# A routed layer of seven tiles: from one written engine order to four

## The chip, the core and the metric

One core of a Trainium2 chip runs the whole program. The metric is the device time of one execution in microseconds (us), the median of several runs. Beside it stands one profiled execution, from which every row below is read. TensorE (PE, with its weight loads as PEld), VectorE (DVE), ScalarE (ACT), GpSimd (POOL) and SyncE (SP) each work through a queue of their own in order; semaphores tie the queues together.

## The reference, cut to what matters

Attention comes first, then a dense layer with a softplus, then the layer that the change touches. In it a score decides which tokens are computed at all, a gate sends each of them to one of eight experts, and the expert's output is scaled and added to the token:

```
do_compute = x @ w_skip > 0
xc = x[do_compute]                       # x: 1152 x 512
e_idx = argmax(xc @ w_gate, axis=1)      # 8 experts
gate_w = softmax(xc @ w_gate)[e_idx]
for e in range(8):
    mask = e_idx == e
    h = maximum(xc[mask] @ w1[e], 0)     # w1[e]: 512 x 1024
    y[mask] = gate_w[mask] * (h @ w2[e]) # w2[e]: 1024 x 512
out[do_compute] = xc + y                 # other tokens: out = x
```

## The kernel before, in words

**Tiles.** The routed tokens are put into tiles of 128 that all belong to one expert: T = 0 to 6. Tile 0 is computed inside `passage` (L800), which also works out the routing; tiles 1 to 6 are the loop in `tiles` (L1165). Rests of an expert with few tokens go into two small items, 0 and 1, of 32 tokens each.

**Weights.** A tile's expert has eight chunks of 128 x 1024 words. Chunks 0 to 3 are w1, chunks 4 to 7 are w2; they are loaded into eight fixed buffers `raw[0]` to `raw[7]` by SP (`load_chunk`, L945). The loads of tiles 1 to 6 carry a condition: where a tile has the same expert as the one before it, the instruction is run and its semaphore rises, but nothing is moved. Each `raw[c]` is one buffer for all tiles, so tile T+1's load of chunk c waits until tile T's readers of it are done.

**Splits.** Products are made exact by splitting each operand into a rounded part and a rest. `split_w` (L962) makes from `raw[c]` a tile `ws` of two halves: ACT casts the rounded part (L966, "cast"), DVE subtracts it to get the rest (L967, "low"). Chunk 0 is not split (`AS_IS`): it is multiplied as it stands, so its matmuls wait for the load of `raw[0]` itself.

**One tile.** Its tokens are fetched by an indirect DMA from POOL into `xg`, turned by four PE transposes (`gather`, L982: `xgt`), copied out by ACT (`xgw`, `xgT`) and DVE (`xgT`, low). The hidden phase multiplies by chunks 0 to 3 into `mh` (4 + 18 matmuls). ACT applies the relu (`hs`, L1022). PE turns `hs` in two halves (`ht`), which ACT and DVE split into `hT`. The result phase multiplies `hT` by chunks 4 to 7 into `y` (24 matmuls). DVE scales and adds (`yo`, L1059), and POOL scatters the rows (L1060); DVE makes its row numbers first (`si`, L1057). In the loop the result of tile T-1 stands behind the hidden phase of tile T.

**Small items.** `small_x` (turn the tokens, `sxt`), `small_hidden` (`smh`, 32 matmuls), `small_turn` (`sht`), `small_result` (`sy`, 64 matmuls; then `ssi`, L1121, and `syo` on DVE). Their weights go through four buffers `sraw`, loaded twice per item, 2 MB each time, without a condition. `SMALL` (L40) says at which tile each step stands.

**What sets the order.** `passage` runs under a manual schedule for PE, DVE, ACT and SP: the written order is the queue's order. `tiles` runs under a manual schedule for PE alone; DVE, ACT and SP are ordered by the scheduler of the language from a timeline that it estimates. `issue_after` pins a few of them. PSUM tiles `xgt`, `ht`, `sxt` and `sht` share two buffers (`ps_x`).

## Time and profile before

| | us |
|---|---|
| median of 3 runs | 516.83 (516.09 to 518.12) |
| profiled execution, its own time | 516.66 |
| its span in the trace | 514.9 |
| between span and time | 1.76 |
| tile 1's first matmul, from the span's start | 397.71 |
| last small result's end, last tile's result begins | 500.4 |

The profiled execution is 0.17 us under the median, so sums are made against it. Columns: a window row gives its bounds and length, then per engine busy us and instructions, the mean granted TensorE clock (1.00 is 2.4 GHz, 0.50 is 1.2 GHz), the DMA share and GB/s. A timeline row gives start, duration, engine, line, operation, output<-input, shapes and count; in brackets stand the idle time before it and what ended that. A wait row gives who waited for whom: us in total, times, the longest.

### The profile page before, as it was taken

Reading aid. Unit: us, or ns where it says so; the run is one execution under the profiler, and the core shown is the slowest. Engines: PE = TensorE matmul, PEld = TensorE weight load, DVE = VectorE, ACT = ScalarE, POOL = GpSimd, SP = SyncE. Lnnn points to the kernel's source line nnn. Section 1 sums busy time; section 2 is a strip of 40 time slices with the busy share of each in tenths; the row PEclk is TensorE's granted clock in tenths of the full one; section 3 lists DMA queues with packets and bytes.
Section 4 is the critical chain, followed back from the end, with each engine's and each line's share of the span. In section 5 each row is a group of like instructions: output and inputs, shape, how many; then the busy total and the mean of one; then the engine's idle time right before and its main releaser. Section 6 shows DMA issues by size and latency. Waiting matters only on the chain. (4 is left out here: it accounts for less than half of the span.)

```text
span 514.9 us, 8832 instructions
## 1 busy us (share of the span) xinstructions
PE 479.5 (93%) x3048; PEld 385.3 (75%) x3049; DVE 371.0 (72%) x697; ACT 331.1 (64%) x782; POOL 122.1 (24%) x167
## 2 busy tenths in 40 slices
PE   7999999998999999999999999999999589799893
PEld 3778777776676788999988998998975456577582
DVE  7676777689987977899898864468847347476882
ACT  2666776767766877877777767666734165464860
POOL 0966967565113200000000000011005200211111
PEclk9999999999999999999999999999999798899997
DMA  7568536746730412233333305003265841909001
GB/s 184 157 167 216 138 89 172 180 127 172 189 97 23 164 42 53 71 123 122 123 123 106 115 27 204 1 4 113 76 204 175 342 164 31 357 30 341 3 25 37
DMA packets 41509, 65.49 MB, mean 127 GB/s; under 512 B 9087, under 2 KB 23679, under 8 KB 41456
## 3 DMA queue, kind: packets, MB, share of 16 engines
q1 hardware_dynamic: 38480, 59.99, 38.1%
q0 software_dynamic: 1344, 4.20, 2.3%
q10 hardware_dynamic: 1632, 0.66, 0.6%
q8 instruction: 26, 0.43, 0.3%
q14 instruction: 27, 0.22, 0.1%
HBM read 67.32 MB, written 6.76 MB: 144 GB/s over the span
## 5 line engine op out<-in xcount | busy, mean ns | idle before, releaser
L590 PE MATMUL h<-xh,w 128*128 128x320 f32 (+2 forms) x464 | 104.2, 309 | 0.8 <-ACT rb L95 0.8
L628 PE MATMUL acc<-w,gh 128*128 128x512 f32 x288 | 80.7, 397 | 1.0 <-ACT gh L618 1.0
L590 PEld LDWEIGHTS h<-xh,w 128*128 128x128 f32 x464 | 78.1, 188 | 4.7 <-ACT rb L95 1.1
L590 PE MATMUL h<-xl,w 128*128 128x320 f32 (+2 forms) x232 | 69.2, 308 | 0.0
L269 DVE TENSOR_REDUCE m<-s 128x1 f32<-128x576 f32 x64 | 48.0, 754 | 19.9 <-PE s L260 16.2
L628 PEld LDWEIGHTS acc<-w,gh 128*128 128x128 f32 x288 | 51.8, 188 | 11.5 <-ACT gh L618 2.7
L967 DVE TENSOR_TENSOR ws<-raw,ws 128x1024 fp32r<-128x1024 f32 x42 | 49.9, 1220 | 7.8 <-ACT ws L966 7.3
L282 ACT ACTIVATE P<-s,m 128x576 f32<-128x576 f32 x64 | 47.6, 750 | 12.2 <-DVE m L269 11.9
L603 ACT ACTIVATE y<-h 128x320 f32<-128x320 f32 (+2 forms) x58 | 25.4, 438 | 41.1 <-PE h L590 39.9
L637 PE MATMUL y<-ws,hT 128*128 128x512 f32 x144 | 40.9, 427 | 8.5 <-ACT ws L966 6.1
L702 POOL TENSOR_SCALAR sc<-lg 128x2 f32<-128x2 f32 (+1 forms) x3 | 0.9, 291 | 201.3 <-DVE lg L685 201.3
L351 PE MATMUL t<-ct,P 128*128 128x128 f32 x288 | 45.6, 277 | 2.5 <-ACT pt L95 2.5
L628 PE MATMUL acc<-w,gl 128*128 128x512 f32 x144 | 45.9, 392 | 0.0
L260 PE MATMUL s<-ks,qs 128*128 128x288 f32 x224 | 43.7, 317 | 1.8 <-ACT P L282 1.8
L590 PEld LDWEIGHTS h<-xl,w 128*128 128x128 f32 x232 | 43.2, 188 | 2.1
L619 DVE TENSOR_TENSOR gl<-r,gh 128x256 fp32r<-128x256 f32 (+2 forms) x42 | 25.8, 614 | 26.1 <-ACT gh L618 25.9
L966 ACT CAST ws<-raw 128x1024 fp32r<-128x1024 f32 x42 | 42.1, 1066 | 3.0 <-issue 3.0
L637 PE MATMUL mh<-ws,xgT 128*128 128x512 f32 x132 | 37.8, 431 | 5.4 <-DVE ws L967 4.4
L351 PEld LDWEIGHTS t<-ct,P 128*128 128x128 f32 x288 | 33.6, 140 | 9.6 <-issue 3.5
L95 ACT COPY pt<-t 128x384 f32<-128x384 f32 x60 | 28.1, 480 | 18.4 <-PE t L351 18.2
L637 PEld LDWEIGHTS y<-ws,hT 128*128 128x128 f32 x144 | 27.2, 200 | 16.3 <-ACT ws L966 6.8
L395 PE MATMUL pv<-pt,vr 128*64 128x256 f32 (+1 forms) x256 | 37.1, 412 | 0.0
(305 smaller groups left out, 945.4 us busy)
## 6 DMA issues: line engine op xcount, KB each, us to landing
raw<-in_moe_w_dram SPq DMA_DIRECT2D x56, 512.0 KB
raw<-in_moe_w_in_dram SPq DMA_DIRECT2D x16, 512.0 KB
raw<-in_moe_w_out_dram SPq DMA_DIRECT2D x16, 512.0 KB
sraw<-in_moe_w_dram SPq DMA_DIRECT2D x16, 512.0 KB
ks<-kT SPq DMA_DIRECT2D x28, 288.0 KB
qs<-qT SPq DMA_DIRECT2D x28, 128.0 KB
wr<-in_moe_w_dram SPq DMA_DIRECT2D x5, 512.0 KB
x2d<-x SPq DMA_DIRECT2D x9, 256.0 KB
```

Of the source, the lines that this page charges most:

```text
L95: self.nc.scalar.copy(out, in_)
L260: nc.tensor.matmul(ps[:, c, 0:288], lhsT=qs[:, a, uc], rhs=ks[:, a, x, 288 * c : 288 * c + 288], start=x == 0, stop=x == 1,)
L269: self.last = nc.vector.tensor_reduce(st["m"][:, a : a + 1], st["ps"][a][:, :, 0:288], axis=AX.XY, op=ALU.max, negate=True)
L282: nc.scalar.activation(P[:, 576 * a : 576 * a + 576].rearrange("p (c n) -> p c n", c=2), ps[:, :, 0:288], AF.Exp, bias=m[:, a : a + 1], ac ...
L351: self.tail = nc.tensor.transpose(ps[:, 128 * i : 128 * i + 128], src, ident)
L395: nc.tensor.matmul(ps[r, 0:n], lhsT=v, rhs=pt[:, k, 0:n], start=i < 0, stop=i == 3, skip_group_check=True,)
L590: nc.tensor.matmul(ps[c][:, 0:m], lhsT=w[:, 0, x, 128 * k : 128 * k + 128], rhs=src[:, k, c0 + m * c : c0 + m * c + m], start=z == 0, stop ...
L619: self.last = nc.vector.tensor_sub(gl, r, gh.bitcast(F32))
L628: nc.tensor.matmul(acc[t], lhsT=g[x][:, 128 * j : 128 * j + 128], rhs=w[:, 1, y, :], start=f == f0 and z == 0, stop=f == f1 and z == 2,)
L637: mm()
L966: hi = nc.scalar.copy(w[:, 0], raw)
L967: self.did[T, c] = hi.ins, nc.vector.tensor_sub(w[:, 1], raw, w[:, 0].bitcast(F32)).ins
```

## The change

`tiles` is put under the manual schedule of all four engines, and its body is rewritten so that every cast, low, load and copy has a written place. The casts and lows of chunks 1 and 2 of tile T+1 and of chunks 5 to 7 of tile T-1 stand during tile T's hidden phase ahead of the relu, chunk 3 of T+1 behind it, chunk 4 of T in the middle of the result phase. The loads follow in the order in which their buffers come free: 5, then 0 of the next tile, 6 and 7, then 1 to 3 of the tile after the next, then 4 of the next. `passage` loads chunks 1, 2, 0 ahead of the routing's values and 3 and 4 behind, and takes over the first splits of tile 1. The transposes of the next tile's tokens (`rows`) move from behind the hidden phase into it, ahead of chunk 3; `gather` is cut into `rows` (PE) and `copies` (ACT and DVE). Tile 1's `ht` halves stand inside tile 2's hidden phase. The small items' tokens and hidden products come one tile later (tiles 2 and 5), the hidden product behind the result phase there; the turned product and result of item 0 move to tile 3, those of item 1 stay at tile 6. The row numbers `ssi` are made with their `syo`. The first loads of item 0 move into tile 1, those of item 1 into tile 4. `yo` and `si` of a tile are written behind the next hidden phase's matmuls. The fetched tokens of a small item get two buffers. The small helpers are cut in the same way into a PE part and a copy.

```diff
@@ -35,7 +35,7 @@
 FAR = 4096.0
 
 FULL = 7
-SMALL = {1: ("x0", "h0"), 2: ("t0", "r0"), 4: ("x1", "h1"), 6: ("t1", "r1")}
+SMALL = {1: ("l0",), 2: ("x0", "h0"), 3: ("t0", "r0"), 4: ("l1",), 5: ("x1", "h1"), 6: ("t1", "r1")}
...
 AS_IS = (0,)
-EARLY_RAW = 2
+EARLY_RAW = (1, 2, 0)
...
@@ -923,12 +923,13 @@
 
         v.tensor_scalar(self.e[:, ST:], ps, 0.0, c["far"], op0=ALU.is_equal, op1=ALU.mult)
         v.tensor_scalar(self.e[:, ST:], self.e[:, ST:], float(self.G), c["part"], op0=ALU.mult, op1=ALU.add)
-        for k in range(EARLY_RAW):
+        for k in EARLY_RAW:
             self.load_chunk(self.raw[k], 0, k)
-        e, new = self.values(1)
-        for k in range(EARLY_RAW, 5):
+        self.values(1)
+        for k in (3, 4):
             self.load_chunk(self.raw[k], 0, k)
-        self.load_w(e, 0, cond=new)
+        self.load(1, 1, 2, 3, 0, 4)
+        self.split_w(1, 1, 2, low=False)
 
         y(7, 0, 0)
         v.tensor_sub(ht[:, 1, 0:512], pt[0], ht[:, 0, 0:512].bitcast(F32))
...
@@ -941,7 +942,9 @@
         v.tensor_sub(w[6][:, 1], self.raw[6], w[6][:, 0].bitcast(F32))
         st = self.gather(1, xp, ps_x)
         y(6, 0, 1)
-        return st, (e, new), partial(self.finish, 0, xg, py, xp)
+        self.split_w(1, 3, low=False)
+        self.low_w(1, 1, 2, 3)
+        return st, partial(self.finish, 0, xg, py, xp)
 
...
             src = self.w2[es, k : k + 256, :].rearrange("o (j p) n -> p (o j) n", p=128)
             queue.dma_start(r.rearrange("p (j n) -> p j n", j=2), src, **kw)
 
-    def load_w(self, e, part, **kw):
-
-        for c in range(4 * part, 4 * part + 4):
-            self.load_chunk(self.raw[c], e, c, **kw)
-
-    def split_w(self, T, c, raw=None):
-        nc = self.nc
-        raw = self.raw[c] if raw is None else raw
-        wp, n = self.ring[2 if c > 3 and (T, c) != (0, 4) else 0 if (c < 1 if T == 0 else (3 * T + c - 4) % 6 < 2) else 1]
-        w = wp.tile([128, 2, 2, 512], F32R, name=f"ws{T}{c}", tag="w", bufs=n).rearrange("p x a n -> p x (a n)")
-        hi = nc.scalar.copy(w[:, 0], raw)
-        self.did[T, c] = hi.ins, nc.vector.tensor_sub(w[:, 1], raw, w[:, 0].bitcast(F32)).ins
-        return w
+    def split_w(self, T, *cs, raw=None, low=True):
+        for c in cs:
+            wp, n = self.ring[2 if c > 3 and T else 0 if (c < 1 if T == 0 else (3 * T + c - 4) % 6 < 2) else 1]
+            w = wp.tile([128, 2, 2, 512], F32R, name=f"ws{T}{c}", tag="w", bufs=n)
+            self.w[T, c] = w.rearrange("p x a n -> p x (a n)")
+            self.nc.scalar.copy(self.w[T, c][:, 0], self.raw[c] if raw is None else raw)
+            if low:
+                self.low_w(T, c, raw=raw)
+
+    def low_w(self, T, *cs, raw=None):
+        for c in cs:
+            w = self.w[T, c]
+            self.nc.vector.tensor_sub(w[:, 1], self.raw[c] if raw is None else raw, w[:, 0].bitcast(F32))
+
+    def load(self, T, *cs):
+
+        e, new = self.reg[T]
+        for c in cs:
+            self.load_chunk(self.raw[c], e, c, cond=new)
 
     def fetch(self, T, xp):
 
...
-        xg = self.xg["s", n] = xp.tile([128, ROW], F32, name=f"sxg{n}", tag="sxg", bufs=1)
+        xg = self.xg["s", n] = xp.tile([128, ROW], F32, name=f"sxg{n}", tag="sxg", bufs=2)
...
     def values(self, T):
 
-        e = self.nc.sync.value_load(self.ei[0:1, T : T + 1], min_val=0, max_val=7)
-        new = self.nc.sync.value_load(self.ei[0:1, 24 + T : 25 + T], min_val=0, max_val=1)
-        return e, new
-
-    def next_w(self, T):
-        e, new = self.values(T)
-        self.load_w(e, 0, cond=new)
-        return e, new
+        self.reg[T] = (
+            self.nc.sync.value_load(self.ei[0:1, T : T + 1], min_val=0, max_val=7),
+            self.nc.sync.value_load(self.ei[0:1, 24 + T : 25 + T], min_val=0, max_val=1),
+        )
...
@@ -1167,74 +1194,107 @@
 
 
         Ts, prev, sm = list(Ts), None, {}
+        last, done = Ts[-1], []
         if start:
-            st, nxt, first = start
+            st, end = start
+            done.append(end)
         else:
-            first, nxt = None, self.next_w(Ts[0])
+            self.values(Ts[0])
+            self.load(Ts[0], 1, 2, 3, 0, 4)
             self.fetch(Ts[0], xp)
+            self.split_w(Ts[0], 1, 2, 3)
             st = self.gather(Ts[0], xp, ps_x)
         for T in Ts[1:3]:
             self.fetch(T, xp)
-
-        def load(n):
-            self.small_load(n, 0)
-            self.small_fetch(n, xp)
-
-        def steps(T, what):
-            for n in (0, 1):
-                if f"{what}{n}" not in small.get(T, ()):
-                    continue
-                if what == "x":
-                    sm[n] = self.small_x(n, xp, ps_x)
-                elif what == "h":
-                    sm[n] = self.small_hidden(n, sm[n], xp, ps_a)
-                    self.small_load(n, 1)
-                elif what == "t":
-                    sm[n] = self.small_turn(n, sm[n], xp, ps_x)
-                else:
-                    self.small_result(n, sm[n], xp, ps_a)
-                    if n == 0:
-                        load(1)
-
-        if small:
-            load(0)
+        self.values(Ts[1])
+        self.load(Ts[1], 1, 2, 3)
+
+        def step(T, what):
+
+            for x in small.get(T, ()):
+                if x[0] == what:
+                    return int(x[1])
+
         for T in Ts:
-            cur = nxt
+            if (n := step(T, "l")) is not None:
+                self.small_load(n, 0)
+                self.small_fetch(n, xp)
             pool, tag = ps_h[T % 2]
             ph = [pool.tile([128, 512], F32, name=f"mh{T}{c}", tag=tag) for c in range(2)]
             mms = self.hidden_mm(T, st, ph)
-            some(mms, 14)
-            steps(T, "x")
+            some(mms, 8)
+            if T == Ts[1]:
+
+                half(0)
+            some(mms, 6)
+            if T == Ts[1]:
+                half(1)
+            if (n := step(T, "x")) is not None:
+                sx = self.small_x(n, ps_x)
+            rows = self.rows(T + 1, ps_x) if T < last else None
             some(mms)
+            if (m := step(T, "t")) is not None:
+                turned = self.small_turn(m, sm[m], ps_x)
+            if prev:
+                for do in done:
+                    do()
+                done = []
+                self.split_w(T - 1, 5, 6, 7)
+            if T < last:
+                self.split_w(T + 1, 1)
+                if prev:
+                    self.split_w(T + 1, 2)
+                else:
+                    self.split_w(T + 1, 2, low=False)
+                if n is not None:
+                    sm[n] = self.small_copy(n, sx, xp)
+                following = self.copies(T + 1, xp, rows)
             st = self.relu(T, st, xp, ph)
-            with ExitStack() as order:
-                if first:
-
-                    for done in self.did[1, 1]:
-                        order.enter_context(self.tc.issue_after(done))
-                    first()
-                    first = None
-                if T + 1 in Ts:
-                    nxt = self.next_w(T + 1)
-                    following = self.gather(T + 1, xp, ps_x)
-            if T + 3 in Ts:
+            if m is not None:
+                sm[m] = self.small_copied(m, turned, xp)
+            if T < last:
+                if not prev:
+                    self.low_w(T + 1, 2)
+                for do in done:
+                    do()
+                done = []
+                self.split_w(T + 1, 3)
+                if not prev:
+                    self.split_w(T, 4)
+            if T + 3 <= last:
                 self.fetch(T + 3, xp)
-            steps(T, "h")
-            steps(T, "t")
+            self.load(T, 5)
+            if T < last:
+                self.load(T + 1, 0)
+            self.load(T, 6, 7)
+            if T + 2 <= last:
+                self.values(T + 2)
+                self.load(T + 2, 1, 2, 3)
             st, half = self.turn(T, st, xp, ps_x)
-            mms = iter(())
-            if prev:
-                py = ps_y.tile([128, 512], F32, name=f"y{T - 1}", tag="y")
-                mms = self.result_mm(T - 1, prev, py)
-            for c in range(2):
-                some(mms, 6)
-                half(c)
-            some(mms)
-            if prev:
-                self.finish(T - 1, prev[0], py, xp)
-            steps(T, "r")
-            self.load_w(cur[0], 1, cond=cur[1])
+            if T > Ts[0] or T == last:
+                mms, py = iter(()), None
+                if prev:
+                    py = ps_y.tile([128, 512], F32, name=f"y{T - 1}", tag="y")
+                    mms = self.result_mm(T - 1, prev, py)
+                for c in range(2):
+                    some(mms, 6)
+                    half(c)
+                if T > Ts[0]:
+                    self.split_w(T, 4)
+                some(mms)
+                if prev:
+                    done.append(partial(self.finish, T - 1, prev[0], py, xp))
+            if T < last:
+                self.load(T + 1, 4)
+            if n is not None:
+                sm[n] = self.small_hidden(n, sm[n], xp, ps_a)
+                self.small_load(n, 1)
+            if m is not None:
+                done.append(self.small_result(m, sm[m], xp, ps_a))
             prev, st = st, following
+        for do in done:
+            do()
+        self.split_w(T, 5, 6, 7)
         pool, tag = ps_h[(T + 1) % 2]
         py = pool.tile([128, 512], F32, name=f"y{T}", tag=tag)
         some(self.result_mm(T, prev, py))
...
         with tc.manual_schedule(engines={nc.tensor.engine, nc.vector.engine, nc.scalar.engine, nc.sync.engine}):
-        with tc.manual_schedule(engines={nc.tensor.engine}):
+        with tc.manual_schedule(engines={nc.tensor.engine, nc.vector.engine, nc.scalar.engine, nc.sync.engine}):
             moe2.tiles(range(1, FULL), xp, *ps, start=start, small=SMALL)
```

What moves, at the three places that the prediction speaks of. Names are those of the program: `raw3` is the buffer of chunk 3, `ws23` the split of tile 2's chunk 3, `mh20` the first half of tile 2's hidden sums.

SP, from the first loads in `passage` to the first loads of `tiles`; before:

```order
L950 DMA raw0_4979<-in_moe2_w1_dram 128x1024
L950 DMA raw1_4980<-in_moe2_w1_dram 128x1024
L1155 TENSOR_LOAD ei_5172
...
L950 DMA raw2_4981<-in_moe2_w1_dram 128x1024
L950 DMA raw3_4982<-in_moe2_w1_dram 128x1024
L954 DMA raw4_4983<-in_moe2_w2_dram 128x2x512
...
L950 DMA raw0_4979<-in_moe2_w1_dram 128x1024
...
L950 DMA raw1_4980<-in_moe2_w1_dram 128x1024
...
L950 DMA raw2_4981<-in_moe2_w1_dram 128x1024
...
L950 DMA raw3_4982<-in_moe2_w1_dram 128x1024
...
L950 DMA sraw0_4984<-in_moe2_w1_dram 128x1024
```

The same stretch after:

```order
L953 DMA raw1_4980<-in_moe2_w1_dram 128x1024
L953 DMA raw2_4981<-in_moe2_w1_dram 128x1024
L953 DMA raw0_4979<-in_moe2_w1_dram 128x1024
L1187 TENSOR_LOAD ei_5172
...
L953 DMA raw3_4982<-in_moe2_w1_dram 128x1024
L957 DMA raw4_4983<-in_moe2_w2_dram 128x2x512
...
L953 DMA raw1_4980<-in_moe2_w1_dram 128x1024
...
L953 DMA raw2_4981<-in_moe2_w1_dram 128x1024
...
L953 DMA raw3_4982<-in_moe2_w1_dram 128x1024
...
L953 DMA raw0_4979<-in_moe2_w1_dram 128x1024
...
L957 DMA raw4_4983<-in_moe2_w2_dram 128x2x512
```

The second load of each buffer is tile 1's own, with the condition. Tile 1's load of `raw0` stood first among these and now stands behind that of `raw3`.

DVE, from tile 1's token split on; before:

```order
L997 TENSOR_TENSOR xgT11_5225<-xgt1_5219,xgT10_5224 128x384
L967 TENSOR_TENSOR ws11_5264<-raw1_4980,ws11_5264 128x1024
L1057 TENSOR_TENSOR si0_5301<-xg0_4421,e0_4414 128x1
L1059 SCALAR_TENSOR_TENSOR yo0_5303<-y0_5069,xg0_4421 128x512
L1057 TENSOR_TENSOR si1_5515<-xg1_5121,e_5119 128x1
L1121 SCALAR_TENSOR_TENSOR ssi0_5555<-sxg0_5256,e_5119 128x1
L967 TENSOR_TENSOR ws12_5273<-raw2_4981,ws12_5273 128x1024
L967 TENSOR_TENSOR ws13_5289<-raw3_4982,ws13_5289 128x1024
```

After:

```order
L1013 TENSOR_TENSOR xgT11_5230<-xgt1_5224,xgT10_5229 128x384
L971 TENSOR_TENSOR ws11_5206<-raw1_4980,ws11_5206 128x1024
L971 TENSOR_TENSOR ws12_5208<-raw2_4981,ws12_5208 128x1024
L971 TENSOR_TENSOR ws13_5237<-raw3_4982,ws13_5237 128x1024
L971 TENSOR_TENSOR ws21_5318<-raw1_4980,ws21_5318 128x1024
L1013 TENSOR_TENSOR xgT21_5324<-xgt2_5307,xgT20_5323 128x384
L971 TENSOR_TENSOR ws22_5321<-raw2_4981,ws22_5321 128x1024
L1073 TENSOR_TENSOR si0_5333<-xg0_4421,e0_4414 128x1
L1075 SCALAR_TENSOR_TENSOR yo0_5335<-y0_5069,xg0_4421 128x512
```

The row numbers of small item 0 (`ssi0`) stood ahead of the lows of chunks 2 and 3 and are gone from here; tile 0's `yo0` has moved behind five lows.

ACT, around tile 2's relu (`hs2`); before:

```order
L1022 ACTIVATE hs2_5418<-mh20_5387 128x512
L1022 ACTIVATE hs2_5418<-mh21_5388 128x512
L995 COPY xgw3_5450<-xgt3_5443 128x128
L996 CAST xgT30_5448<-xgt3_5443 128x384
L1103 COPY shT0_5461<-sht0_5458 128x256
L966 CAST ws14_5465<-raw4_4983 128x1024
L966 CAST ws15_5481<-raw5_4976 128x1024
```

After:

```order
L1053 CAST hT1_5375<-ht10_5387 128x512
L1053 CAST hT1_5375<-ht11_5400 128x512
L964 CAST ws15_5423<-raw5_4976 128x1024
L964 CAST ws16_5426<-raw6_4977 128x1024
L964 CAST ws17_5429<-raw7_4978 128x1024
L964 CAST ws31_5432<-raw1_4980 128x1024
L964 CAST ws32_5435<-raw2_4981 128x1024
L1100 COPY sxT0_5438<-sxt0_5407 128x128
L1011 COPY xgw3_5442<-xgt3_5412 128x128
L1012 CAST xgT30_5440<-xgt3_5412 128x384
L1038 ACTIVATE hs2_5446<-mh20_5377 128x512
L1038 ACTIVATE hs2_5446<-mh21_5378 128x512
```

The cast of tile 1's chunk 4 (`ws14`) stood behind the relu and now stands two rows ahead of this piece; five casts and the token copies now stand ahead of the relu.

## Rows read from the trace of the kernel before

**Rows 1.** The page's part 1: busy us, share, instructions of each engine.

```profile
PE 479.5 (93%) x3048; PEld 385.3 (75%) x3049; DVE 371.0 (72%) x697; ACT 331.1 (64%) x782; POOL 122.1 (24%) x167
```

**Rows 2.** Windows: tile 4 and tile 6.

```profile
454.70:470.00 15.30, 15.30 (x95) 11.18 (x94) 12.09 (x15) 10.76 (x16) 1.74 (x1) 1.00 0.46 158
485.90:500.40 14.50, 14.50 (x121) 11.06 (x119) 12.12 (x15) 10.71 (x14) 1.71 (x1) 1.00 0.06 21
```

**Rows 3.** Waits of PE, 394 to 515 us.

```profile
PE y L637 <- ACT ws L966: 6.1, 3, 2.1
...
PE mh L637 <- DVE ws L967: 4.4, 1, 4.4
...
PE y L637 <- DVE ws L967: 2.4, 3, 1.3
...
PE mh L637 <- ACT ws L966: 0.9, 1, 0.9
```

**Rows 4.** Timeline of PE, 397 to 464 us.

```profile
397.71 1.91 PE L637 MATMUL mh<-raw,xgw 128*128 128x512 f32 x4
...
407.50 1.22 PE L637 MATMUL mh<-ws,xgT 128*128 128x512 f32 x2 [4.38 <-DVE ws L967]
...
425.39 0.73 PE L637 MATMUL y<-ws,hT 128*128 128x512 f32 x2 [2.09 <-ACT ws L966]
...
436.30 1.98 PE L637 MATMUL mh<-raw,xgw 128*128 128x512 f32 x4
...
442.32 0.60 PE L986 MATMUL xgt<-ct,xg 128*128 128x128 f32 x4
...
461.57 1.93 PE L1089 MATMUL smh<-sraw,sxT 128*32 128x256 f32 x32
463.43 1.67 PE L637 MATMUL y<-ws,hT 128*128 128x512 f32 x6
```

**Rows 5.** Timeline of DVE, 406 to 450 us.

```profile
406.12 0.16 DVE L1121 SCALAR_TENSOR_TENSOR ssi<-sxg,e 128x1 int32<-128x1 f32 x1 [5.16 <-DMA sxg<-x2d,gi]
...
445.75 3.49 DVE L967 TENSOR_TENSOR ws<-raw,ws 128x1024 fp32r<-128x1024 f32 x3
```

**Rows 6.** Timeline of ACT: a cast in tile 1, and around tile 3's relu.

```profile
400.83 1.04 ACT L966 CAST ws<-raw 128x1024 fp32r<-128x1024 f32 x1 [1.93 <-issue]
...
442.35 1.08 ACT L1022 ACTIVATE hs<-mh 128x512 f32<-128x512 f32 x2 [7.18 <-PE mh L637]
...
443.46 0.51 ACT L996 CAST xgT<-xgt 128x384 fp32r<-128x384 f32 x1
443.83 2.97 ACT L966 CAST ws<-raw 128x1024 fp32r<-128x1024 f32 x3
```

**Rows 7.** Timeline of SP's queue, single issues, 394 to 418 us.

```profile
394.88 0.32 SPq L950 DMA_DIRECT2D raw<-in_moe_w_dram  x1
...
396.51 0.11 SPq L950 DMA_DIRECT2D raw<-in_moe_w_dram  x1
...
400.76 0.07 SPq L950 DMA_DIRECT2D raw<-in_moe_w_dram  x1
403.06 0.02 SPq L950 DMA_DIRECT2D raw<-in_moe_w_dram  x1
403.25 0.89 SPq L950 DMA_DIRECT2D sraw<-in_moe_w_dram  x2
...
416.49 0.48 SPq L954 DMA_DIRECT2D raw<-in_moe_w_dram  x2
```

**Rows 8.** Windows of PE with its granted clock, around four stalls.

```profile
403.00:417.00 14.00, 9.62 (x60) 0.76 0.67 242
422.00:432.00 10.00, 7.38 (x32) 0.83 0.01 2
442.00:453.00 11.00, 7.63 (x32) 0.84 0.81 308
476.00:486.00 10.00, 7.49 (x38) 1.00 0.01 5
```

More of the change, by code (lines that the diff above doesn't have):

```diff
@@ L660, in __init__ @@
         self.tok = rp.tile([128, 9, 1], F32, name="tok")
-        self.xg, self.did = {}, {}
+        self.xg, self.w, self.reg = {}, {}, {}
         self.lg = rp.tile([128, 9, 9], F32, name="lg")
@@ L802, in passage @@
         nc, c, ST, SS, sb = self.nc, self.cst, self.ST, self.SS, self.sp
-        w = {4: self.early[4]}
+        w = {4: self.w[0, 4]}
         def high(k):
@@ L981, in gather, with rows @@
     def gather(self, T, xp, ps_x, tag="x"):
+        return self.copies(T, xp, self.rows(T, ps_x, tag))
+    def rows(self, T, ps_x, tag="x"):
         nc, ident = self.nc, self.cst["ident"]
@@ L986, in gather, with copies @@
             nc.tensor.transpose(ps[:, 128 * k : 128 * k + 128], xg[:, 128 * k : 128 * k + 128], ident)
+        return ps
+    def copies(self, T, xp, ps):
+        nc, xg = self.nc, self.xg[T]
         xt = [
@@ L1009, in hidden_mm @@
                 continue
-            w = self.early[k] if T == 0 else self.split_w(T, k)
+            w = self.w[T, k]
             for z, (x, y) in enumerate(((0, 0), (1, 0), (0, 1))):
@@ L1044, in result_mm @@
         for c in range(4):
-            w = self.split_w(T, 4 + c)
+            w = self.w[T, 4 + c]
             for j in range(2):
@@ L1071, in small_load, with small_x @@
             self.load_chunk(self.small_raw[c], self.es, 4 * part + c)
-    def small_x(self, n, xp, ps_x):
-        nc, SM = self.nc, self.SM
+    def small_x(self, n, ps_x):
         xg = self.xg["s", n]
@@ L1077, in small_x, with small_copy @@
         for k in range(4):
-            nc.tensor.transpose(ps[:, 128 * k : 128 * k + 128], xg[:, 128 * k : 128 * k + 128], self.cst["ident"])
-        xt = xp.tile([128, 4, SM], F32, name=f"sxT{n}", tag="sx", bufs=1)
-        nc.scalar.copy(xt, ps.rearrange("p (k m) -> p k m", k=4)[:, :, 0:SM])
+            self.nc.tensor.transpose(
+                ps[:, 128 * k : 128 * k + 128], xg[:, 128 * k : 128 * k + 128], self.cst["ident"]
+            )
+        return ps
+    def small_copy(self, n, ps, xp):
+        xt = xp.tile([128, 4, self.SM], F32, name=f"sxT{n}", tag="sx", bufs=1)
+        self.nc.scalar.copy(xt, ps.rearrange("p (k m) -> p k m", k=4)[:, :, 0 : self.SM])
         return xt
@@ L1095, in small_hidden, with small_turn, small_copied @@
         return hs
-    def small_turn(self, n, hs, xp, ps_x):
-        nc, w = self.nc, FE // self.G
+    def small_turn(self, n, hs, ps_x):
         ps = ps_x.tile([128, 512], F32, name=f"sht{n}", tag="x")
-        for j in range(w // 128):
-            nc.tensor.transpose(ps[:, 128 * j : 128 * j + 128], hs[:, 128 * j : 128 * j + 128], self.cst["ident"])
+        for j in range(FE // self.G // 128):
+            self.nc.tensor.transpose(
+                ps[:, 128 * j : 128 * j + 128], hs[:, 128 * j : 128 * j + 128], self.cst["ident"]
+            )
+        return ps
+    def small_copied(self, n, ps, xp):
+        w = FE // self.G
         ht = xp.tile([128, w], F32, name=f"shT{n}", tag="sht", bufs=1)
-        nc.scalar.copy(ht, ps[:, 0:w])
+        self.nc.scalar.copy(ht, ps[:, 0:w])
         return ht
@@ L1118, in small_result, with small_finish @@
                 )
-        o = self.ST + n
+        return partial(self.small_finish, n, py, xp)
+    def small_finish(self, n, py, xp):
+        nc, SM, G, w = self.nc, self.SM, self.G, DM // self.G
+        xg, o = self.xg["s", n], self.ST + n
         si = xp.tile([128, 1], I32, name=f"ssi{n}", tag="si", bufs=3)
@@ L1139, in small @@
         self.small_fetch(n, xp)
-        hs = self.small_hidden(n, self.small_x(n, xp, ps_x), xp, ps_a)
+        xt = self.small_copy(n, self.small_x(n, ps_x), xp)
+        hs = self.small_hidden(n, xt, xp, ps_a)
         self.small_load(n, 1)
-        self.small_result(n, self.small_turn(n, hs, xp, ps_x), xp, ps_a)
+        ht = self.small_copied(n, self.small_turn(n, hs, ps_x), xp)
+        self.small_result(n, ht, xp, ps_a)()
     def small_fetch(self, n, xp):
-        xg = self.xg["s", n] = xp.tile([128, ROW], F32, name=f"sxg{n}", tag="sxg", bufs=1)
+        xg = self.xg["s", n] = xp.tile([128, ROW], F32, name=f"sxg{n}", tag="sxg", bufs=2)
         o = self.ST + n
@@ L1439, in attention_moe_moe_kernel @@
                     moe2.load_chunk(raw, 0, c)
-                    moe2.early.append(moe2.split_w(0, c, raw))
+                    moe2.split_w(0, c, raw=raw)
                 if (ph, f) == XGT:
```

3 lines of the change are left out of this document (2 added, 1 removed).

## Prediction

> **What bounds the kernel now.** I read the page's first part, then windows by tile, then PE's waits, then the queues of the engines named there. PE is busy 93% of the span [rows 1], so only its gaps and its clock can pay. Tiles 4 and 6 show what a tile costs when PE never waits: 15.30 us with a small item's `sxt` and `smh`, 14.50 us with `sht` and `sy`, the clock at 1.00 and PE busy throughout [rows 2]. DVE is busy 12.1 of those 15.3 us and ACT 10.8, so neither bounds a tile by amount. From tile 1 on PE waits 6.1 + 4.4 + 2.4 + 0.9 = 13.8 us, all of it for casts and lows of weights [rows 3]. So the splits come late by their order, not by their amount.
>
> Two patterns make these waits. The largest, 4.38 us ahead of 407.50 [rows 4], is for a low in tile 1: DVE was free, but in its queue `ssi` stood ahead and waited 5.16 us for the fetched tokens of a small item [rows 5]. The other is a gap of about 2 us behind the hidden phase, three times in all, once ahead of 425.39 [rows 4]: at tile 3 ACT did the relu (442.35), the token copies (to 443.83) and only then the cast that PE wanted [rows 6].
>
> The gaps also cost clock. Behind the first, the window 403 to 417 has a mean clock of 0.76, so 14 x 0.24 = 3.4 us lost; 0.83 over 10 us and 0.84 over 11 us lose 1.7 and 1.8 us; behind a fourth gap, 476 to 486, nothing [rows 8]. Gaps and clock together are 13.8 + 6.9 = 20.7 us of the 102.7 us from 397.71 to 500.4. That is the most the change could give; the work itself is the same matmuls.
>
> **The change part by part.** I lay PE's new queue out from 397.71 on, with durations from the rows.
>
> *The unit prices.* Hidden phase: 442.32 - 436.30 = 6.0 us [rows 4]. Four transposes: 0.4 us (0.60 with the drain that the next matmul covers, an estimate). `smh`: 463.43 - 461.57 = 1.86. A result phase with its two `ht` runs from 463.43 to 470.00 (the end of tile 4's window): 6.57 [rows 2, 4]; a quarter without `ht` is (6.57 - 0.8)/4 = 1.45. A bare tile is 15.30 - 0.4 - 1.86 = 13.05. A cast is 2.97/3 = 0.99, a low 3.49/3 = 1.16, half a relu 0.54, token copies 0.51 [rows 5, 6]. An issue on SP that moves data has a pitch of about 0.45 to 0.55, one whose condition is off about 0.4 (two begun within 0.48) [rows 7].
>
> *Tile 1's start gets worse.* Tile 1's matmuls on `raw0` wait for tile 1's own load of it. It stood first, at 396.51; now it stands behind tile 1's load of `raw3`, which overwrites a buffer still being filled and so waits for the first `raw3` to land. SP's queue holds everything behind it. Before, the first chunk issued behind the routing's values (394.88) landed when its successor could issue, 400.76, the second at 403.06 [rows 7]. `raw3` now has that first place, so I take 400.76, and `raw0` goes at 401.2. PE stands from 397.75 to 401.2: 3.5 us of new stall. The bounds of the landing: with nothing beside it a chunk takes at most the 2.3 us between 400.76 and 403.06, so 397.2 at the earliest, and no stall; 403.06, one place later, at the latest, and 2.3 us more.
>
> *The rest of tile 1 is covered.* Casts of chunks 1 and 2 run at 396.5 to 398.5, `xgw` behind them, the lows by 402.0, chunk 3's cast at 401.9 and low at 403.2; PE wants them from 402.6 on. `ssi` no longer stands in DVE's queue, so the 4.38 us go. Hidden phase and `xgt`: 401.2 + 6.4 = 407.6. Tile 2's `raw0` on SP: `raw4` lands at 403.1, three loads with the condition off to 404.3, a value load 0.6, four real `sraw` issues to 406.9, two more to 407.5. Level with PE; no stall.
>
> *Tile 2 keeps a stall.* PE: hidden phase with two `ht`, `sxt` and `xgt`, 7.6 us, and about 0.9 us for `xgt` to get its PSUM buffer back from tile 1's second `hT` low: 416.1. A quarter of the result: 417.55. Then `ht` of tile 2 wants the relu. ACT: tile 1's second `ht` ends on PE at 412.8, its copy at 413.35, five casts 4.95, three token copies 0.65, half a relu 0.54: 419.5. So PE waits 1.9 us, about the 2.09 that it waited there for the cast [rows 4]. The remaining 5.1 us of the result and `smh` 1.86 bring tile 3 to 426.5; before, it began at 436.30 [rows 4].
>
> *Tiles 3 to 6 run free.* From a tile's second `ht`, ACT needs 0.55 + 0.99 (chunk 4) + 4.95 + 0.65 + 0.54 = 7.7 us to the next relu, and PE gets to that relu's `ht` only after half a result, a hidden phase and a quarter: 2.9 + 6.4 + 1.45 = 10.75. That is 3 us of slack, and the three 2 us gaps go. The tightest place is tile 3, where ACT waits for `smh` before its five casts: the lows end some 0.3 us ahead of PE. The loads of tile 4, the ones that move data, now issue during tile 2 and 3 instead of one tile ahead; a 2 MB item (some 6 us at 242/0.67 = 361 GB/s, an estimate from [rows 8]) fits beside them. So tile 3 costs 14.5 + 0.4 = 14.9 (it has `sht`, `sy` and also `xgt`), tile 4 13.05, tile 5 15.3, tile 6 14.5: 57.75 us, and `sy` ends at 484.25 instead of 500.4. The end behind it stays 14.5 us, from 500.4 [rows 2] to the span's 514.9: the last lows now stand behind `syo` on DVE and cost PE some 0.7 us, hidden by the scatters that follow one another there. Span without any clock loss: 498.75.
>
> *Clock.* Two stalls stay, 3.5 and 1.9 us. Three of four such gaps brought a half-clock stretch of 1.7 us or more loss [rows 8], so I take both: 3.4 us. Span 502.15, and with the 1.76 us around it **503.9 us**, 12.8 us under 516.66.
>
> *Two rules against this.* A load whose condition is off took SP 0.07 us at 400.76, and ACT's cast of that chunk began at 400.83 [rows 6, 7]. The Trainium skill, DMA: Bandwidth & Descriptors, "Anatomy of one DMA", gives about 2.0 us fixed for every DMA, mostly completion; by it each skipped load would release its reader 2 us later, tile 1 would start 2 us later, and the estimate from that page would be 505.9. It rests on transfers that happen; the row decides here. The other rule is a rival, below.
>
> **The rivals.**
>
> *A: as forecast, two clock losses.* 503.9; with a double loss behind the first stall, as at 403 to 417, 505.6.
>
> *B: fewer clock losses.* The fourth gap of [rows 8] lost nothing. With one loss 502.2, with none 500.5. For it: the stalls are shorter than 4.38 us; against: three of four lost.
>
> *C: more waits than I found.* At tile 3 the slack is 0.3 us, at tile 2 several queues meet within 1 us, and `raw3` may land 2.3 us later. Two more stalls of 1 to 2 us with one loss of 1.7 are 3.7 to 5.7 us: 507.6 to 509.6.
>
> *D: slower than before.* Written queues couple the engines: if ACT's five casts each wait for their chunk (SP holds a load until a low, the low stands behind casts), the relu comes late in every tile as in tile 2. The price is 1.9 + 1.7 = 3.6 us in each of tiles 3 to 6, 14.4 us: 518.3. It decides once the casts wait more than the 3 us of slack per tile. Against it: SP's loads with the condition off take 0.4 us, and only tile 4 moves data.
>
> *E: the repeated gap is a buffer.* The gap of some 2 us comes back three times because a split's buffer is freed late, so the new order cannot remove it: the three gaps and their lows stay, 6.1 + 2.4 = 8.5 us [rows 3], of which the forecast keeps 1.9, and two more clock losses of 1.7 come: 503.9 + 6.6 + 3.4 = 513.9. Against it: at 443.83 the cast starts the moment that ACT is done with the copies [rows 6], so it waited for ACT, not for a buffer. The Trainium skill says in Perfetto Trace Analysis, "Identifying Performance Opportunities", that a gap repeating on the engine that should be full can mean too few SBUF or PSUM buffers; by that rule the time is E's. The trace does not bear it out.
>
> *F: the change doesn't do what it says.* The scheduler's order might have been the written one already: 516.7. The rows of the queues show otherwise at all three places.
>
> **How the numbers follow.** A 0.48, B 0.17, C 0.20, D 0.06, E 0.04, F 0.02, and 0.03 for a gain too small to tell, as a C with several more stalls. About 0.5% is what a measurement of this kernel can tell from no change, so faster is under 514.2: A, B, C and half of E, 0.87; the same 0.07 (F, the small gain, the other half of E); slower 0.06 (D). The likeliest is 503.9. The range takes in B's lower end with `raw3` landing a little earlier and C's upper end: 499.5 to 511.
>
> **What would show it.** Tile 1's `raw0` matmuls start near 401 and wait for a DMA; no wait for `ssi` on DVE; tile 3 starts near 428; a wait of `ht` for ACT's `hs` in tile 2 and none in tiles 4 to 6; tiles 4 and 5 at 13 and 15.3 us; half clock for some 3 us behind each of two stalls; `sy` ends near 488. Wrong if the lows of tile 3 come late, if ACT waits for loads inside its casts, or if the 2 us gap returns.

## The result and the profile after

The changed kernel takes 503.41 us, median of 4 runs (503.4 to 504.41), against 516.66 before (516.09 to 518.12): ratio 0.9744, 95% interval 0.9721 to 0.9768. The forecast was 503.9. The profiled execution took 503.40 us with a span of 501.3 and a mean clock of 0.992; before, 516.66, 514.9 and 0.981.

The page's part 1 answers [rows 1]: PE is busy 5.0 us less, though the matmuls are the same; that is about what is gone of the half clock, under which the same four matmuls took 3.63 us at 401.12 and 1.99 us at 428.46 (6.9 us were lost to it by [rows 8], 1.7 us now, read below).

```profile
PE 474.5 (95%) x3049; PEld 381.9 (76%) x3049; DVE 370.6 (74%) x697; ACT 331.5 (66%) x782; POOL 121.6 (24%) x167
```

What fell is waiting and half clock. PE's waits from 394 us on (who waits for whom: us in total, times, longest) answer [rows 3]:

```profile
PE mh L637 <- DMA raw<-in_moe_w_dram: 2.8, 1, 2.8
PE ht L1051 <- ACT hs L1038: 1.8, 1, 1.8
PE y L637 <- DVE ws L971: 1.4, 1, 1.4
PE xgt L998 <- DVE hT L1054: 1.0, 1, 1.0
```

7.0 us where there were 13.8. The 4.4 us for a low in tile 1 and the three gaps of some 2 us for casts are gone; a wait for `raw0` is new. PE's timeline from there on answers [rows 4] (start, us, engine, line, operation, idle before it and its releaser in brackets; the rows on `raw` are the starts of tiles 1 to 3):

```profile
401.12 3.63 PE L637 MATMUL mh<-raw,xgw 128*128 128x512 f32 x4 [2.76 <-DMA raw<-in_moe_w_dram]
...
409.23 1.88 PE L637 MATMUL mh<-raw,xgw 128*128 128x512 f32 x4
...
416.17 0.66 PE L998 MATMUL xgt<-ct,xg 128*128 128x128 f32 x4 [0.96 <-DVE hT L1054]
...
421.39 0.66 PE L1051 MATMUL ht<-ct,hs 128*128 128x128 f32 x4 [1.77 <-ACT hs L1038]
...
428.46 1.99 PE L637 MATMUL mh<-raw,xgw 128*128 128x512 f32 x4
...
490.16 4.00 PE L637 MATMUL y<-ws,hT 128*128 128x512 f32 x16 [1.35 <-DVE ws L971]
```

Tiles 3 to 6, each from its first matmul to the next tile's (bounds, length, busy PE, PEld, DVE, ACT, POOL, clock, DMA share, GB/s), answer [rows 2]:

```profile
428.46:443.86 15.40, 15.29 (x129) 11.52 (x125) 10.79 (x13) 12.90 (x19) 2.07 (x3) 1.00 0.59 206
443.86:456.79 12.93, 12.93 (x63) 9.94 (x60) 11.17 (x14) 7.56 (x12) 1.39 (x2) 1.00 0.91 350
456.79:472.00 15.21, 15.21 (x96) 11.02 (x94) 11.60 (x15) 8.74 (x13) 2.44 (x2) 1.00 0.05 16
472.00:486.68 14.68, 14.68 (x125) 11.21 (x121) 6.93 (x9) 9.52 (x13) 1.00 (x2) 1.00 0.44 164
```

PE is busy 58.11 of these 58.22 us at full clock; before, tiles 3 to 6 (436.30 to 500.4) took 64.1, without the first small item's turned product and result, which tile 3 now holds as well. The windows around the two stalls of tiles 1 and 2 answer [rows 8], the clock being the third number from the end:

```profile
397.00:403.00 6.00, 3.13 (x10) 1.57 (x10) 4.35 (x5) 3.17 (x5) 4.78 (x5) 0.84 0.97 347
403.00:409.00 6.00, 6.00 (x25) 4.23 (x24) 1.64 (x3) 2.64 (x4) 0.99 (x1) 0.88 0.77 247
...
421.00:427.00 6.00, 5.61 (x34) 4.37 (x38) 5.55 (x8) 3.79 (x6) 0.00 (x0) 1.00 0.65 252
```

Behind the first stall 6 x 0.16 + 6 x 0.12 = 1.7 us are lost to half clock, behind the second nothing. DVE makes `ssi` at 442.75, beside `syo`, and waits for nothing there; in [rows 5] it stood at 406.12 and waited 5.16.

### The profile page after: what moved, and what is told of

Its sections match the earlier page's. It is cut to its first block, busy times and chain, and to the rows that moved or that the text cites. A ratio compares the mean times of both kernels' runs of the same rounds, so it can differ in the third digit from the quotient of the medians.

```text
span 501.3 us, 8831 instructions
## 1 busy us (share of the span) xinstructions
PE 474.5 (95%) x3049; PEld 381.9 (76%) x3049; DVE 370.6 (74%) x697; ACT 331.5 (66%) x782; POOL 121.6 (24%) x167
## 5 line engine op out<-in xcount | busy, mean ns | idle before, releaser
L637 PE MATMUL y<-ws,hT 128*128 128x512 f32 x144 | 37.5, 403 | 1.4 <-DVE ws L971 1.4
L260 PEld LDWEIGHTS s<-ks,qs 128*128 128x128 f32 x224 | 31.6, 189 | 6.5 <-ACT P L282 3.6
```

The source lines that it names most:

```text
L260: nc.tensor.matmul(ps[:, c, 0:288], lhsT=qs[:, a, uc], rhs=ks[:, a, x, 288 * c : 288 * c + 288], start=x == 0, stop=x == 1,)
L637: mm()
```

## The experiments

Times are medians; each group of four ran beside the kernel before on one chip, and a ratio is to that kernel. Single executions of one variant of the changed kernel differ by up to 3.6 us (e1_raw0_first: 501.25 to 504.81), so for effects under 2 us the trace decides. Only one execution of each kernel has a trace, so where the others differ from it is not shown.

**Why tile 1 waits for `raw0`.** e1_raw0_first:

```diff
-        self.load(1, 1, 2, 3, 0, 4)
+        self.load(1, 0, 1, 2, 3, 4)
```

> The changed kernel with one thing different: tile 1's own load of raw0 stands first of its five loads on SP, not fourth. Theory Queue (tile 1's first matmuls wait only because raw0's load stands behind raw3's on SP): the 2.76 us wait for a DMA ahead of 401.12 goes, tile 1 starts near 398.4, and the half-clock stretch behind it (1.65 us) goes too. But tile 2's raw0 load still issues at 407.7, so PE now waits there for a DMA, some 3 us, and tile 2 starts at 407.8 instead of 409.23: gain 1.4 us, 502.0 us, or about 503.6 if a half-clock stretch follows the new wait. Rival Chunk (raw0's data land late, the place on the queue does not matter): the wait at 401 stays, 503.4 us.

503.47 us, ratio 0.9745 (0.9721 to 0.9769): in the medians nothing. The trace is of the fastest of the five (501.25), which has no half clock behind its stalls; the mean clocks of the others go from 0.998 down to 0.992. In it the wait moved as theory Queue said, and is smaller at its new place:

```profile
398.83 1.99 PE L637 MATMUL mh<-raw,xgw 128*128 128x512 f32 x4 [0.92 <-ACT xgw L1011]
...
406.97 1.96 PE L637 MATMUL mh<-raw,xgw 128*128 128x512 f32 x4 [1.52 <-DMA raw<-in_moe_w_dram]
```

From tile 0's last result matmuls (397.18 here, 397.64 in the changed kernel) to the span's end it is 102.0 us instead of 103.7. Chunk falls: the data were there at 398.83.

e2_raw0_both adds tile 2's load of `raw0` ahead of the small item's loads:

```diff
         self.load(Ts[1], 1, 2, 3)
+        if start:
+            self.load(Ts[1], 0)
...
-            if T < last:
+            if T < last and not (start and T == Ts[0]):
                 self.load(T + 1, 0)
```

> As the run before it, and tile 2's load of raw0 also stands ahead of the small item's four loads on SP. Theory Queue: neither tile 1 nor tile 2 waits for raw0; the 2.76 us wait and its 1.65 us of clock are gained whole, tile 2 starts near 404.8 instead of 409.23, and the time is 499.0 us. Rival Chunk: 503.4 us. Rival Next wait (ACT's casts and DVE's lows of tiles 1 and 2 become late when PE comes earlier): part of the gain is given back, 500.5 to 502.5 us, with longer waits for ws in tile 1 or 2.

508.26 us, 0.983 (0.9807 to 0.9853): all three theories miss. The edit was not the one meant. It writes tile 2's load ahead of tile 1's matmuls on the same buffer, so tile 1 must wait for that load too (and multiplies by tile 2's chunk 0, the same one here, since both tiles have one expert). SP's issues (x3: chunks 2, 3 and 0 of tile 2), then PE:

```profile
403.28 0.86 SPq L953 DMA_DIRECT2D raw<-in_moe_w_dram  x3
```

```profile
404.26 3.75 PE L637 MATMUL mh<-raw,xgw 128*128 128x512 f32 x4 [5.77 <-DMA raw<-in_moe_w_dram]
```

The last issue takes 0.07 us and ends at 404.14; PE starts 0.12 us later. A load that moves nothing still costs its reader the whole of its place in the queue: 5.77 us.

e3_both_ssi puts `ssi` (now made in `small_rows`) ahead of two lows of tile 1 on top of that:

```diff
-        self.low_w(1, 1, 2, 3)
+        self.low_w(1, 1)
...
                 self.small_fetch(n, xp)
+                if n == 0:
+                    self.small_rows(n, xp)
+                    self.low_w(1, 2, 3)
```

> As the run before it, and DVE computes the small item's scatter rows ssi early again, ahead of the lows of tile 1's chunks 2 and 3, as it stood in the kernel before. Theory Queue (ssi held DVE's queue, and that was the largest wait of the kernel before): DVE waits for sxg until about 405.4 to 406.1, PE waits some 4 us for the low of chunk 2 in tile 1, with one half-clock stretch of 1.7 us behind it: 504.7 us, between 503.0 without and 506.4 with two clock losses. Rival (ssi was incidental, and the lows come in time anyhow): as the run before it, 499.0 us.

507.76 us, 0.9824 (0.9797 to 0.9851), the same as e2_raw0_both. This tells nothing of `ssi`: PE stood until 405.11 for `raw0`, and DVE's wait lay beneath that. Both were made again.

**The same, as meant.** e5_raw0_clean issues tile 2's load behind tile 1's two matmuls on `raw0`:

```diff
-            some(mms, 8)
+            some(mms, 2)
+            early = start and T == Ts[0]
+            if early:
+                self.load(T + 1, 0)
+            if (n := step(T, "l")) is not None:
+                self.small_load(n, 0)
+                self.small_fetch(n, xp)
+            some(mms, 6)
```

> The changed kernel with tile 1's load of raw0 first of its five, and with tile 2's load of raw0 issued behind tile 1's matmuls on raw0 but ahead of the small item's four loads (in the second run it had been written ahead of those matmuls, so that tile 1 had to wait for it). Counted from the last result matmuls of tile 0, where the changed kernel needed 103.7 us to the span's end and the first run 102.0. Theory Queue: tile 1 waits for xgw at most 0.9 us, tile 2 not at all for raw0 and starts 1.5 us sooner than in the first run, 100.5 us to the end, 500.2 us in all. Rival Next wait (what ACT and DVE split for tiles 1 and 2 becomes late): tile 2's part is given back, 102 us, 501.8 us.

499.95 us, 0.968 (0.9657 to 0.9703), as theory Queue had it. Tile 2 starts at 406.02 with no wait, the clock stays at 1.00 from 397 to 433, and the waits left are the old ones and the one for `xgw`:

```profile
PE ht L1051 <- ACT hs L1038: 1.8, 1, 1.8
PE y L637 <- DVE ws L971: 1.4, 1, 1.4
PE xgt L998 <- DVE hT L1054: 1.0, 1, 1.0
PE mh L637 <- ACT xgw L1011: 0.9, 1, 0.9
```

**What `ssi` cost.** e6_ssi is e5_raw0_clean with the edit of e3_both_ssi.

> As the run before it, and DVE computes the small item's rows ssi ahead of the lows of tile 1's chunks 2 and 3, as it stood in the kernel before; with tile 1 starting early again nothing hides it. Theory Queue: DVE stands for sxg until about 405.4, PE waits some 3.6 us for the low of chunk 2 in tile 1, and one half-clock stretch may follow: 503.8 us without, 505.5 us with it. Rival (ssi was incidental): as the run before it.

504.14 us, 0.976 (0.9737 to 0.9783): 4.2 us over e5_raw0_clean; the theory said 3.6 to 5.3. DVE, then PE:

```profile
405.06 0.16 DVE L1150 SCALAR_TENSOR_TENSOR ssi<-sxg,e 128x1 int32<-128x1 f32 x1 [3.58 <-DMA sxg<-x2d,gi]
405.13 3.49 DVE L971 TENSOR_TENSOR ws<-raw,ws 128x1024 fp32r<-128x1024 f32 x3
```

```profile
406.41 0.73 PE L637 MATMUL mh<-ws,xgT 128*128 128x512 f32 x2 [2.66 <-DVE ws L971]
```

A 0.16 us instruction whose input comes late holds two lows, and PE 2.66 us; the mean clock is 0.81 in 406 to 415, 1.7 us more in this execution (504.93). In two of the five, the median one among them, the mean clock of the whole is 0.996 instead of 0.993, so the half clock doesn't seem to follow each time. The wait is the pattern of [rows 4, 5], put back by the place of one instruction.

**The wait of tile 2.** e4_relu:

```diff
                 self.split_w(T - 1, 5, 6, 7)
+            if T == Ts[1]:
+                st = self.relu(T, st, xp, ph)
             if T < last:
                 self.split_w(T + 1, 1)
```

> The changed kernel with tile 2's relu moved on ACT from behind the five casts to behind the first three of them. Theory Queue (ht of tile 2 waits 1.77 us only for ACT's order): the wait goes, hs is there near 419.2, tile 3 starts near 426.7 instead of 428.46, 501.6 us. Rival Given back: the casts and token copies behind the relu come 1.1 us later and PE waits for them at tile 3's start or in its result phase: 502.5 to 503.4 us.

504.1 us, 0.9751 (0.9726 to 0.9776): no gain, and neither theory's mechanism. The relu came at 418.77, behind three casts; PE waited all the same. PE's waits, then ACT:

```profile
PE ht L1051 <- ACT sxT L1100: 1.7, 1, 1.7
```

```profile
418.77 1.08 ACT L1038 ACTIVATE hs<-mh 128x512 f32<-128x512 f32 x2
419.74 2.00 ACT L964 CAST ws<-raw 128x1024 fp32r<-128x1024 f32 x2
421.62 0.28 ACT L1100 COPY sxT<-sxt 128x128 f32<-128x128 f32 x1
```

`ht` shares two PSUM buffers with `sxt` and `xgt`, and the copy `sxT` that frees the first stood behind the same casts. In the changed kernel it was done 1.1 us ahead of `ht` (421.39), and the relu came last; with the relu moved in front of it, it comes 1 us later itself. ACT of the changed kernel:

```profile
420.03 0.26 ACT L1100 COPY sxT<-sxt 128x128 f32<-128x128 f32 x1
...
420.71 1.11 ACT L1038 ACTIVATE hs<-mh 128x512 f32<-128x512 f32 x2
```

e7_copies moves the copies too:

```diff
+            first = T == Ts[1]
+            if first:
+                if n is not None:
+                    sm[n] = self.small_copy(n, sx, xp)
+                following = self.copies(T + 1, xp, rows)
+                st = self.relu(T, st, xp, ph)
             if T < last:
                 self.split_w(T + 1, 1)
```

> The changed kernel with sxT, the token copies and the relu of tile 2 moved together on ACT (and the low of the copies on DVE) from behind five casts to behind the first three. In the run e4_relu the relu alone was moved, and PE waited the same 1.7 us, now put down to sxT, whose copy frees a PSUM buffer that ht needs. Theory Buffer (the wait at tile 2 has two equal causes, the relu and the PSUM buffer that the copy behind the casts frees): both gone, PE's 1.8 us wait for ht goes, 101.9 us from the last result matmuls of tile 0 to the end, 501.7 us. Rival Casts (PE will wait for the two casts pushed back, or for their lows, at tile 3): 103.0 us and over, 502.8 us or more.

502.12 us, 0.9719 (0.9695 to 0.9743); from tile 0's last result matmuls (397.83) 102.0 us to the end. PE has no wait for `ht` any more, and tile 3 takes 15.08 us instead of 15.40. Buffer holds in that the relu alone was not enough, but the two causes were not equal: in the changed kernel PE was free for `ht` at 419.62 and the buffer at 420.29, so the buffer alone would have held it 0.7 us, the relu held it 1.77. Moving the relu alone moved nothing because it set the copy back; the copies alone were not moved.

**Which queues matter.** e8_pe_only leaves DVE, ACT and SP in the tiles to the scheduler (first line with +), e10_pe_sp only DVE and ACT (second):

```diff
-        with tc.manual_schedule(engines={nc.tensor.engine, nc.vector.engine, nc.scalar.engine, nc.sync.engine}):
+        with tc.manual_schedule(engines={nc.tensor.engine}):
+        with tc.manual_schedule(engines={nc.tensor.engine, nc.sync.engine}):
             moe2.tiles(
```

> The changed kernel with only TensorE in written order in the tiles, as before; VectorE, ScalarE and SyncE are placed by the scheduler, from the same new code. On SP the scheduler puts eleven value loads, some 0.5 us each, ahead of tile 2's loads; DVE has ssi behind the lows of tile 1 there too. Theory Queue (the gain is in where the splits and loads stand, whoever places them): tile 2's raw0 comes near 412, PE waits some 3 us and loses one half-clock stretch, the other waits stay gone, 506 to 508 us. Rival Written order (only the written queues remove the waits): the repeated 2 us waits for ws are back, 513 to 517 us. Rival New TensorE order alone: 503.4 us.

509.23 us, 0.986 (0.983 to 0.989). Above the range of theory Queue, with its mechanism: on SP ten value loads (eleven were expected) stand between tile 1's last load and tile 2's first, and ACT behind them, and PE behind ACT, wait longer than the 3 us that were expected. SP, then PE:

```profile
404.84 0.07 SPq L957 DMA_DIRECT2D raw<-in_moe_w_dram  x1
411.25 0.98 SPq L953 DMA_DIRECT2D raw<-in_moe_w_dram  x3
```

```profile
415.81 3.75 PE L637 MATMUL mh<-raw,xgw 128*128 128x512 f32 x4 [7.42 <-ACT hs L1038]
```

ACT's casts of tile 2's chunks wait for those loads and hold the token copies and the relu. Tiles 3 to 6 run as in the changed kernel: 435.76 to the end of `sy` at 493.68 is 57.9 us.

> The changed kernel with TensorE and SyncE in written order and VectorE and ScalarE by the scheduler; against e8_pe_only only SP differs. There SP ran eleven value loads between 404.8 and 411.3 and tile 2 started 6.6 us later than in the changed kernel. Theory SP (the whole of that loss is SP's order): PE's 7.4 us wait at tile 2 goes, 503.4 us, at most 505. Rival (ACT and DVE in the scheduler's order cost as well): 506 us or more.

503.8 us, 0.975 (0.9727 to 0.9773), level with all four queues written: theory SP. DVE and ACT in the scheduler's order cost nothing that can be measured. The trace shows a loss and a gain behind this: tile 2 starts 1.7 us later than in the changed kernel (410.95: the stall for `raw0` is 3.3 us, and tile 1 takes 8.8 us, against 8.1 in the changed kernel and 6.45 in e5_raw0_clean, which has no half clock there), and from there to the span's end it is 1.4 us shorter, since neither `ht` in tile 2 nor the last result phase waits.

e9_before_written is the opposite: the code of the kernel before, all four queues written.

```diff
-        with tc.manual_schedule(engines={nc.tensor.engine}):
+        with tc.manual_schedule(engines={nc.tensor.engine, nc.vector.engine, nc.scalar.engine, nc.sync.engine}):
             moe2.tiles(
```

> The kernel before, its code and its TensorE order untouched, with VectorE, ScalarE and SyncE also in the order that its code is written in. There ssi stands behind the lows of tile 1, and each split stands just ahead of the matmuls that use it, in every tile; where the scheduler had moved casts ahead (tiles 4 to 6) they fall back. Theory Place (the gain is in where the new code puts splits and loads, and written queues without it are worth nothing): the 4.4 us wait for ssi goes, with its 3.4 us of clock, but a gap of 2 us or more for a cast comes in each of tiles 2 to 6 and twice in some: 512 to 524 us, slower than or level with before. Rival Queues (written queues alone bring the gain): 503 to 507 us.

568.43 us, 1.0981 (1.093 to 1.1033), far beyond what theory Place allowed, in its direction. Its code writes each split just ahead of the matmuls that use it:

```profile
PE y L637 <- ACT ws L966: 25.7, 15, 2.1
PE y L637 <- DVE ws L967: 7.8, 11, 2.8
```

The expectation counted one such gap in a tile; there are 15 waits for casts and 11 for lows in the result phases of six tiles, and the mean clock falls to 0.937.

**A faster version.** e11_best is e5_raw0_clean with e7_copies and, at the end,

```diff
-        for do in done:
-            do()
+        done[0]()
         self.split_w(T, 5, 6, 7)
+        for do in done[1:]:
+            do()
```

> The changed kernel with the edits of e5_raw0_clean and e7_copies together, and on DVE the lows of the last tile's chunks 5 to 7 ahead of the small item's syo instead of behind it. Theory Sum: 499.95 - 1.75 for the wait of tile 2, and the 1.4 us wait of the last result phase goes, of which the chain of scatters lets some 0.7 us through: 497.5 us. Rival Given back (the waits overlap, or syo comes 3.5 us later and the scatter behind it sets the end): 498.2 to 500.5 us.

497.0 us (496.52 to 497.16), 0.962 (0.9601 to 0.9638), nearest to theory Sum: 3.8% faster than before, 1.3% than the changed kernel. The wait of the last result phase is gone; from the end of `sy` to the span's end it is 13.7 us instead of 14.6, so 0.9 of the 1.35 us came through. On POOL the scatter of `syo` now waits for DVE's queue, and the last scatter starts 3.14 us behind it:

```profile
485.34 0.98 POOL L1159 DMA_INDIRECT out_dram<-syo,ssi  x1 [3.10 <-DVE si L1073]
488.48 0.99 POOL L1076 DMA_INDIRECT out_dram<-yo,si  x1 [2.16 <-DVEq L1553]
```

e12_best2 also casts chunk 2 of tile 1 behind `xgw` and turns `ht` of tile 1 sooner:

```diff
-        self.split_w(1, 1, 2, low=False)
+        self.split_w(1, 1, low=False)
...
-        self.split_w(1, 3, low=False)
+        self.split_w(1, 2, 3, low=False)
...
-            some(mms, 6)
+            some(mms, 3)
             if T == Ts[1]:
 
                 half(0)
-            some(mms, 6)
+            some(mms, 5)
             if T == Ts[1]:
                 half(1)
+            some(mms, 4)
```

> As the run before it, with two waits more taken away: ACT's copy xgw of tile 1 ahead of the cast of chunk 2 (0.86 us at tile 1's start), and the two ht of tile 1 after 5 and 10 matmuls of tile 2 instead of 8 and 14, so that their PSUM buffers are free when xgt of tile 3 wants one (0.96 us). Theory Sum: 495.7 us, PE without a wait over 0.3 us in tiles 1 to 5. Rival: the casts of chunks 2 and 3 or the relu of tile 1 now come late, and 0.5 to 2 us of it are given back, 496.2 to 498 us.

497.1 us (495.88 to 498.36), 0.9616 (0.9593 to 0.9639): the same as e11_best. In the profiled execution, the slowest of its five, the wait for `xgt` of tile 3 (0.7 us in e11_best) is gone, the one at tile 1's start is 0.5 us instead of 0.7, and a wait of 2.0 us for tile 2's `xgw` is there. ACT:

```profile
406.27 1.99 ACT L964 CAST ws<-raw 128x1024 fp32r<-128x1024 f32 x2 [2.89 <-DMA raw<-in_moe_w_dram]
408.17 0.26 ACT L1011 COPY xgw<-xgt 128x128 f32<-128x128 f32 x1
```

The casts stand ahead of the copy and wait for tile 2's loads, which SP holds until tile 1's `raw4` has landed: 405.76 here, 403.20 in e11_best. Whether the two fastest runs (495.88) are those in which it landed early was not profiled.

## Why the prediction was right, and where it was not

| step | forecast | measured |
|---|---|---|
| tile 1 starts | 401.2 | 401.12 |
| stall ahead of it | 3.5 | 2.76, tile 0 ending 0.6 later |
| tile 2 starts, with one clock loss | 407.6 + 1.7 = 409.3 | 409.23 |
| `xgt`, then `ht` wait in tile 2 | 0.9, 1.9 | 0.96, 1.77 |
| tile 3 starts, without clock | 426.5 | 428.46 - 1.7 = 426.8 |
| tiles 3 to 6 | 57.75 | 58.22 |
| from `sy` to the span's end | 14.5 | 14.6 |
| clock losses | 3.4 | 1.7 |
| around the span | 1.76 | 2.1 |

498.75 + 0.3 + 0.5 + 0.1 + 1.7 = 501.3, the span.

*Tile 1's start* was right in time and cause. That the queue holds `raw0`, and not its data, is shown by e1_raw0_first and e5_raw0_clean. Keeping it cost 503.41 - 499.95 = 3.5 us: the stall and its clock, 4.4 us, less the 0.9 us for `xgw` that PE waits there in its place. The skipped load releases its reader at once: the trace shows 0.12 us in e2_raw0_both. The Trainium skill, DMA: Bandwidth & Descriptors, "Anatomy of one DMA", gives about 2.0 us fixed per DMA, mostly for the completion, for the path through GpSimd (the prediction told it of every DMA, wider than the page has it); of a load on SP whose condition is off that section says nothing, so the measurement decides.

*`ssi`* was right: 4.2 us come back with it. e3_both_ssi shows that they only do so when nothing larger stands over them.

*The clock* is the term that was mis-sized: rival A's two losses were taken as the likeliest, rival B's one came. The span's other terms were 0.9 us over the forecast and the time around it 0.3, so the total was only 0.5 us off by the luck of errors that cancel; by its working it is B's 502.2 that should be compared, 1.2 us under the measured time. Of the 3.4 us that the prediction read behind the 4.38 us gap, 0.4 lie inside the gap: half clock was granted from 406.7 on, and PE began at 407.50.

*Tile 2's stall* had the right size and the right last cause, but the prediction put the second cause at nothing. It named the relu behind five casts; e4_relu and e7_copies show that the copy `sxT` behind the same casts, which frees a PSUM buffer, has to come sooner as well. Rival E, that a gap is a buffer, was refused at tile 3 by its row, and the repeated gaps did go; here it holds for the first 0.7 us. The Trainium skill, Perfetto Trace Analysis, "Identifying Performance Opportunities", reads a gap that repeats on the engine that should be full as a possible lack of buffers: for the repeated gaps the trace disagrees; this gap does not repeat, and a buffer has a part in it.

*Tile 3* took 15.40 us instead of 14.9: where it does not wait it takes 15.08 (e7_copies), so 0.2 us are its price and 0.3 us a short wait ahead of `ht` at 436.77, which starts as the copy `shT` ends (436.71). The lows that the prediction feared there did not hold PE. *The tail's* wait was put at 0.7 us and hidden; it was 1.35, and e11_best shows that 0.9 of it was not hidden.

*Rival D*, slower by coupled queues, did not come, but e8_pe_only shows its mechanism in one tile (casts that wait for loads hold the relu, 7.4 us). *Where the gain is from:* the new code with PE and SP in written order is enough (e10_pe_sp); the written order of DVE and ACT adds nothing, and written queues as such are no gain (e9_before_written). By the traces it is the places of the splits: before, ACT stood idle for 7.18 us ahead of tile 3's relu with the cast behind it [rows 6]; in the changed kernel (430.10 to 434.93) and in e10_pe_sp (426.41 to 431.51) it runs five casts ahead of that relu, and PE does not wait for a cast behind it. But the change also gave PE a new order, and no run has the old order of PE with the new places or the other way round, so their shares stay open.

## What to carry to other kernels

Look at what stands ahead in the queue, not at the engine's load: a 0.16 us instruction with a late input, or ten register loads on SP, cost 4 to 5.5 us each. Before moving an instruction that PE waits for, list everything that has to be done by then, PSUM buffers too, since moving one cause can set back the next. A written order is worth what its places are worth: the new code, with its splits far ahead and a new order of PE, gave 2.6%; the old code, with its splits just in time, lost 10% by it.
